# One accumulation for tokens k and 768-k: a shared second DFT, mirrored tiles, and their stores

## The chip, the cores and the metric

The kernel runs on one core of one Trainium2 chip. The metric is the device time of one execution in microseconds (us), some 1.8 us more than the profile's span. Times are medians over several executions. On one core the fast state is recognised by comparison with the other runs of the same kernel; two runs of the kernel before, one at 391.51 us with a granted clock of 0.667 (in the round of experiment 9) and one at 294.96 us (experiment 10), fell in the slow state and are not used in any ratio.

In the views, PE is TensorE (matmuls) and PEld its weight loads, DVE is VectorE, ACT ScalarE, POOL GpSimd, and SP the engine that issues the plain stores; SPq is its queue of DMAs. A bank is a part of PSUM, the memory in which matmuls accumulate. The granted clock (PEclk) is the share of TensorE's full clock that the profile shows as granted. A scatter is a store that takes the address of each row from a table. To land is to be complete in memory.

## The reference, cut to what matters

The first part is attention over blocks that a Sinkhorn-normalised matrix mixes (4 batches, 8 heads, 768 tokens, 64 columns a head). Its output x, 768 tokens of 512 columns per batch, goes through this:

```python
    X = np.fft.fft(x, axis=1)            # over 768 tokens
    X = np.fft.fft(X, axis=2)            # over 512 columns
    u = x + np.real(X)
    un = (u - mean(u)) / sqrt(var(u) + 1e-06)          # per token
    return u + np.maximum(un @ w_ch1, 0.0) @ w_ch2     # 512 -> 2048 -> 512
```

The real part has a symmetry: X[768-k, m] is X[k, 512-m]. Tokens k and 768-k therefore have the same spectrum with its columns reversed.

## The kernel before

A Python list scheduler fixes the order on every engine before launch, from cost estimates that each operation is added with. The 768 tokens are six tiles of 128 rows; tiles 0 to 2 are group 0 and tiles 3 to 5 are group 1, and a group goes through the MLP as one. Each tile has a buffer u that lives from the second DFT, through the statistics and the MLP, to the store of the result; there are six, so the next batch's u can be written only when this batch's store has landed.

```python
    many("u", 6, [128, DM], F32)                # six u buffers
    P.pool("pf", banks[0:5])                    # PSUM: five banks, and three for the MLP
    P.pool("pm", banks[5:8])
    ...
    def dft2(b, g):
        ...
        for tt in range(3):
            T = 3 * g + tt
            ps, u, st = Buf("pf"), Buf("u"), Buf("st")
            ...
            def f(_, one=one, ps=ps, T=T):
                for c in range(4):
                    one(c)                                        # 4 matmuls of 256 columns
                nc.tensor.matmul(ps.ap, lt[:, 128 * T:128 * T + 128], rb,
                                 start=False, stop=True, ...)     # 1 of 512 columns
            P.add(pe(mm(256, 4) + mm(512) + 0.05), f, ..., w=[ps, u], tag="dft2")
            P.add({"DVE": (0.6, 0.69)}, ... V.scalar_tensor_tensor(u ... rt ... ps),  tag="u")
            # then bn_stats and bn_aggr on DVE, four small operations on POOL ("ln"),
            # then un on DVE or ACT, its transpose by DMA, and the MLP of the group

    def mlp(b, g, pr_pe, pr_v):
        ...                                    # 16 blocks: 4 matmuls of 384 columns, then relu
        for tt in range(3):
            ...                                # 16 matmuls of 512 columns into one bank
            P.add({"DVE": (0.6, 0.69)}, lambda _, u=u, ps=ps:
                  V.tensor_tensor(u.ap, ps.ap, u.ap, op=ALU.add), ..., tag="res")
            P.add({"SP": (0.1, 2.3)}, lambda _, u=u, T=3 * g + tt:
                  nc.sync.dma_start(out_v[b, T], u.ap), r=[(u, 1)], w=[],
                  prio=pr_v, tag="out")        # 128 rows of 2 KB
```

## Time and profile before

| | before |
|---|---|
| median of 3 runs | 291.64 us (290.91 to 291.75) |
| profiled span, granted clock | 287.7 us, 0.994 |
| matmuls | 2332, TensorE busy 262.3 us |
| landing of a 128-row store | 2.0 us |
| start of the last residual addition to the end | 3.86 us |

The prediction below shows the lines that carry this.

### The profile page before, as it was taken

What the parts mean: (1) busy time and instruction counts of PE and PEld (TensorE: products, weight loads), DVE (VectorE), ACT (ScalarE), POOL (GpSimd) and SP (SyncE); (2) the same over time, 40 slices, a digit from 0 to 9 for tenths busy, and PEclk for the clock granted to TensorE, in tenths of its full rate; (3) what the DMA queues carried; (4) which work ended last, traced back from release to release, by engine and by line L of the source; (5) the groups of instructions that cost most, each with busy time, mean ns of one, the idle gap of its engine ahead of it and who ended that gap; (6) DMA issues with size and microseconds to landing.
All of it is one profiled execution on the core that took longest, in us unless ns stands there. A gap on an engine that the chain in (4) does not pass through costs nothing.

```text
span 287.7 us, 5848 instructions
## 1 busy us (share of the span) xinstructions
PE 262.3 (91%) x2332; PEld 159.9 (56%) x2332; DVE 174.4 (61%) x395; ACT 155.9 (54%) x315; POOL 54.1 (19%) x91
## 2 busy tenths in 40 slices
PE   0489987798999998999999999999999999999994
PEld 0258866655576565544576556456645645645541
DVE  4688999999999979971459863044514314302011
ACT  2688989738779737780369117316803712722700
POOL 8973300014900370200020002000200200200000
PEclk9997999999999999999999999999999999999999
DMA  7999999910991299330111220311111022021102
GB/s 115 220 263 240 214 209 212 218 44 2 151 154 27 21 217 123 63 79 32 48 46 44 13 106 8 54 73 43 46 59 62 9 55 110 11 46 73 39 0 109
DMA packets 43025, 26.32 MB, mean 91 GB/s; under 512 B 29834, under 2 KB 38552, under 8 KB 42996
## 3 DMA queue, kind: packets, MB, share of 16 engines
q0 software_dynamic: 22576, 15.16, 35.0%
q1 hardware_dynamic: 20422, 10.78, 14.1%
q8 instruction: 18, 0.29, 0.4%
q14 instruction: 9, 0.07, 0.1%
HBM read 28.95 MB, written 6.29 MB: 122 GB/s over the span
## 4 chain that ended last, share of the span: by engine, by line
PE 70%; DVE 17%; DMA 6%; issue 2%; ACT 2%; POOL 1%; DVEq 0%; ACTq 0%; POOLq 0%
PE bank L1177 28%; PE bank L1156 26%; DMA hr<-in_v_dram 4%; PE bank L1068 3%; PE bank L1015 3%; DVE rt L964 3%; PE bank L854 2%; DVE vsf L626 2%; DMA out_dram<-u 2%; DVE eb L930 2%; PE bank L1075 2%; PE bank L690 2%; PE bank L909 2%; PE bank L949 1%; DVE pmt L981 1%
## 5 line engine op out<-in xcount | busy, mean ns | idle before, releaser
L1168 ACT ACTIVATE hr<-bank 128x384 f16<-128x384 f32 x112 | 54.9, 490 | 84.0 <-PE bank L1156 83.6
L1156 PE MATMUL bank<-ut,w1sb 128*128 128x384 f16 x512 | 92.2, 326 | 0.0
L1177 PE MATMUL bank<-w2sb,hr 128*128 128x512 f16 x384 | 88.0, 379 | 0.0
L1156 PEld LDWEIGHTS <-w1sb 128*128 128x128 f16 x512 | 48.1, 98 | 32.9
L1177 PEld LDWEIGHTS <-hr 128*128 128x128 f16 x384 | 36.9, 98 | 41.2
L1185 DVE TENSOR_TENSOR u<-bank,u 128x512 f32<-128x512 f32 x24 | 16.5, 689 | 62.2 <-PE bank L1177 62.0
L1083 DVE SCALAR_TENSOR_TENSOR u<-rt,bank 128x512 f32<-128x512 f16 x24 | 16.1, 681 | 30.0 <-PE bank L1075 24.0
L918 ACT ACTIVATE ex<-bank 96x384 f32<-96x384 f32 x64 | 27.9, 487 | 9.8 <-PE bank L909 9.2
L1096 POOL TENSOR_SCALAR mv<-mv 128x3 f32<-128x3 f32 x8 | 2.0, 252 | 160.4 <-DVE mv L1091 148.4
L932 ACT ACTIVATE eb<-ex,negone 96x384 f16<-96x384 f32 x36 | 21.4, 617 | 0.1
L949 PE MATMUL bank<-vsf,eb 97*128 97x65 f16 x384 | 16.4, 193 | 2.6 <-DVE rt L964 1.0
L949 PEld LDWEIGHTS <-eb 97*128 97x128 f16 x384 | 14.8, 97 | 5.2 <-issue 2.2
L964 DVE TENSOR_TENSOR rt<-bank,rz 128x384 f16<-128x384 f32 x32 | 17.5, 550 | 0.3
L442 POOL DMA_DIRECT2D kq<-in_q_dram x20 | 16.4, 846 | 1.7 <-DMA kq<-in_q_dram 1.2
L1089 DVE BATCH_NORM_STATS2 st<-u 128x6 f32<-128x512 f32 x24 | 16.0, 684 | 0.2
L884 PE MATMUL bank<-pack,qr 128*128 128x128 f16 x48 | 4.8, 245 | 12.0 <-ACT qr L626 11.5
L626 ACT CAST vsf<-bank 96x512 f16<-96x512 f32 x16 | 11.9, 793 | 4.1 <-PE bank L690 3.3
L1116 ACT ACTIVATE un<-u,nm,ny 128x512 f16<-128x512 f32 x14 | 11.3, 810 | 3.8 <-DMA ut<-un 2.2
L690 PE MATMUL bank<-bdv,vcx 128*128 128x128 f16 (+1 forms) x128 | 12.5, 225 | 0.1
L854 PE MATMUL bank<-bdk,kq 128*64 128x128 f16 x192 | 10.6, 227 | 2.1 <-DVE bdk L602 0.8
L909 PE MATMUL bank<-qt,ks 64*128 64x96 f16 x256 | 11.4, 207 | 1.2 <-DVE u L1083 0.5
L626 DVE CAST vsf<-bank 96x512 f16<-96x512 f32 x16 | 11.7, 777 | 0.9 <-PE bank L693 0.8
(115 smaller groups left out, 323.8 us busy)
## 6 DMA issues: line engine op xcount, KB each, us to landing
out_dram<-u SPq DMA_DIRECT2D x24, 256.0 KB, 2.0
kq<-in_k_dram POOLq DMA_DIRECT2D x8, 384.0 KB, 6.3
w1sb<-in_moe_w_ch_dram POOLq DMA_DIRECT2D x4, 512.0 KB, 16.0
w2sb<-in_moe_w_ch_dram POOLq DMA_DIRECT2D x4, 512.0 KB, 19.0
kq<-in_q_dram POOLq DMA_DIRECT2D x4, 384.0 KB, 11.5
hr<-in_v_dram POOLq DMA_DIRECT2D x2, 768.0 KB, 11.0
kq<-in_v_dram POOLq DMA_DIRECT2D x2, 768.0 KB, 21.7
kq<-in_q_dram POOLq DMA_DIRECT2D x16, 96.0 KB, 5.7
```

What stands on the lines that cost most here:

```text
L442: o = P.add({eng: c}, lambda _: e.dma_start(dst, src), r=r, w=w, prio=prio, nbytes=nbytes, tag="load", after=after)
L626: (nc.scalar.copy if e == "ACT" else V.tensor_copy)(dst, src)
L690: nc.tensor.matmul(o, vcx[:, 96 * d:96 * d + m], bd, start=True, stop=(t == 1))
L909: nc.tensor.matmul(pss[h2].ap[:, BLK * j:BLK * j + BLK], ks.ap[rows, 4 * g + j, :], qt.ap[rows, c0:c0 + BLK])
L918: nc.scalar.activation(ex.ap, pss[h2].ap[0:96, 0:384], AF.Exp, scale=SCALE),
L932: nc.scalar.activation(ed, src, AF.Identity, bias=negone[0:96])
L949: nc.tensor.matmul(po.ap[:, 65 * T:65 * T + 65], eb.ap[:, e0:e0 + 128], vsf[:, vi:vi + 65], start=(n == 0), stop=(n == 1), skip_group_chec ...
L964: P.add({"DVE": (0.45, 0.56)}, lambda _: V.tensor_tensor(rt.ap[:, :, D * h:D * h + D], po3()[:, :, 0:D], rz.ap[:, :, None].broadcast_to([1 ...
L1156: nc.tensor.matmul(ps.ap[:, 0:GT], w1sb[:, c, 128 * fc:128 * fc + 128], ut.ap[:, c, :], start=(c == 0), stop=(c == 3))
L1168: nc.scalar.activation(hr[g][:, fc, :], ps.ap[:, 0:GT], AF.Relu)
L1177: nc.tensor.matmul(ps.ap, hr[g][:, fc, 128 * tt:128 * tt + 128], w2sb[:, fc, :], start=(fc == 0), stop=(fc == 15))
L1185: V.tensor_tensor(u.ap, ps.ap, u.ap, op=ALU.add),
```

## The change

Its intent is to take work from TensorE. Tiles 3 and 4 hold the mirrors of tiles 0 and 1, row for row, so they need not be accumulated again: one closing matmul, onto the bank that tile 0 or 1 has left in PSUM, exchanges the tokens' own part, and DVE reads that bank with its columns reversed. The first DFT is folded by s and -s, with fewer and longer matmuls. Mirrored rows run downwards in the output, so group 1 is stored by scatter, and tile 2 becomes tokens 257 to 383 and token 0, which is stored in two pieces. The MLP order of the last batch is turned round as well. The core of the diff, with cuts:

```diff
+TOK = [list(range(1, 129)), list(range(129, 257)),
+       list(range(257, 384)) + [0], list(range(767, 639, -1)),
+       list(range(639, 511, -1)), list(range(511, 383, -1))]
 ...
+            if T in (3, 4):
+                ps = banks_of[b, T - 3]
+                def f(_, ps=ps, T=T):
+                    nc.tensor.matmul(
+                        ps.ap, lt[:, LTD + 128 * (T - 3):LTD + 128 * (T - 2)],
+                        rb, start=False, stop=True, skip_group_check=True)
+                P.add(pe(mm(512) + 0.03), f, r=lts, w=[ps, u], tag="dft2")
 ...
+                    rev = bass.AP(
+                        tensor=p_.tensor, offset=p_[:, 511:512].offset,
+                        ap=[p_.ap[0], [-1, 255], [-256, 2]])
 ...
-            P.add({"SP": (0.1, 2.3)}, lambda _, u=u, T=3 * g + tt:
-                  nc.sync.dma_start(out_v[b, T], u.ap), r=[(u, 1)], w=[],
-                  prio=pr_v, tag="out")
+            def f(_, u=u, T=3 * g + tt):
+                t0 = TOK[T][0]
+                if T < 2:
+                    nc.sync.dma_start(out[b, t0:t0 + 128, :], u.ap)
+                elif T == 2:
+                    nc.sync.dma_start(out[b, t0:t0 + 127, :], u.ap[0:127])
+                    nc.sync.dma_start(out[b, 0:1, :], u.ap[127:128])
+                else:
+                    i = 3 * b + T - 3
+                    nc.gpsimd.indirect_dma_start(
+                        out.rearrange("b s m -> (b s) m"),
+                        bass.IndirectOffsetOnAxis(ap=rows[:, i:i + 1],
+                                                  axis=0), u.ap, None)
+            P.add({"SP": (0.1, 2.3)} if g == 0 else {"POOL": (1.2, 3.5)}, f,
+                  r=[(u, 1), "rows"], w=[], prio=pr_v, tag="out")
 ...
-            mlp(b, g, 100.0 + 10 * (2 * b + g), -300.0)
+            mlp(b, g, 100.0 + 10 * (2 * b + (g if b < B - 1 else 1 - g)), -300.0)
```

## The prediction

> **What bounds the kernel now.** I read the page first (engine shares, then the 40 slices), then busy time by stretches, then the chain of waits, then the timeline around one hand-over between batches. Shares and slices:
>
> ```profile
> PE 262.3 (91%) x2332; PEld 159.9 (56%) x2332; DVE 174.4 (61%) x395; ACT 155.9 (54%) x315; POOL 54.1 (19%) x91
> ...
> PE   0489987798999998999999999999999999999994
> ...
> DVE  4688999999999979971459863044514314302011
> ```
>
> The second row is PE, the third DVE: up to slice 16 (about 115 us) DVE is full and PE has holes; from slice 17 on PE is full. The stretches say it in us (PE, PEld, DVE, ACT, POOL):
>
> ```profile
> 40.00:60.00 20.00, 15.57 (x272) 12.74 (x267) 19.87 (x51) 17.67 (x40) 0.00 (x0) 1.00 1.08 198
> ...
> 120.00:140.00 20.00, 20.00 (x152) 10.09 (x150) 9.93 (x20) 10.18 (x22) 0.25 (x1) 1.00 0.21 57
> ...
> 180.00:200.00 20.00, 20.00 (x112) 10.76 (x111) 5.08 (x10) 6.80 (x14) 0.00 (x0) 1.00 0.23 57
> ```
>
> So the end is set by PE work left from about 117 us, provided that nothing keeps PE waiting there. The chain of waits gives the rate of each kind of PE work in that stage (start, us, what, how many):
>
> ```profile
> 155.82 0.91 PE bank L949 x24
> ...
> 191.46 0.44 PE bank L1068 x4
> 192.12 0.44 PE bank L1068 x4
> ...
> 200.36 1.70 PE bank L1015 x18
> ...
> 207.15 7.77 PE bank L1177 x36
> ```
>
> That is attention-times-value (L949) 0.91/24 = 38 ns; second DFT (L1068) 0.44 us for four 256-column matmuls, with 0.66 us from tile to tile, so 0.22 us for the closing 512-column one; first DFT (L1015) 1.70/18 = 94 ns for 193 columns; second MLP layer (L1177) 216 ns.
>
> The hand-over matters most. When the last tile of MLP group (1,0) is stored, its u buffer is refilled by batch 2, and all that normalises batch 2 hangs on that. Timeline of DVE, then POOL, then PE:
>
> ```profile
> 170.50 0.69 DVE L1185 TENSOR_TENSOR u<-bank,u 128x512 f32<-128x512 f32 x1 [0.75 <-PE bank L1177]
> ...
> 174.41 0.69 DVE L1083 SCALAR_TENSOR_TENSOR u<-rt,bank 128x512 f32<-128x512 f16 x1 [1.62 <-PE bank L1075]
> 175.13 0.69 DVE L1089 BATCH_NORM_STATS2 st<-u 128x6 f32<-128x512 f32 x1
> ```
> ```profile
> 176.13 0.23 POOL L1096 TENSOR_SCALAR mv<-mv 128x3 f32<-128x3 f32 x1 [24.98 <-DVE mv L1091]
> ```
> ```profile
> 181.37 7.93 PE L1177 MATMUL bank<-w2sb,hr 128*128 128x512 f16 x36
> 189.13 0.81 PE L1156 MATMUL bank<-ut,w1sb 128*128 128x384 f16 x4
> ```
>
> The refill at 174.41 waited for PE, not for the store, because a store lands fast:
>
> ```profile
> out_dram<-u SPq DMA_DIRECT2D x24, 256.0 KB, 2.0
> ```
>
> And after the last residual add only one such store remains:
>
> ```profile
> 283.84 0.69 DVE L1185 TENSOR_TENSOR u<-bank,u 128x512 f32<-128x512 f32 x1 [2.76 <-PE bank L1177]
> 284.56 0.33 SPq L1188 DMA_DIRECT2D out_dram<-u  x1
> ```
>
> **What the Trainium skill says.** (1) "DMA: Bandwidth & Descriptors", section "Why a DMA increments its semaphore by 16 and not by 1": a DMA runs on the largest k of at most 16 engines that divides the slowest dimensions of both sides, and a 127-partition tile issued from SP gets k = 1. All stores in this trace have 128 rows, so it cannot agree or disagree. (2) The same page, "Specifications": about 27 GiB/s for one engine. The stretch holding only the last store fits:
>
> ```profile
> 284.90:286.70 1.80, 0.00 (x0) 0.00 (x0) 0.00 (x0) 0.00 (x0) 0.00 (x0) 1.00 0.38 146
> ```
>
> 0.38 x 16 engines x 1.8 us = 10.9 engine-us for 128 rows of 2 KB, 85 ns a row, 24 GB/s. (3) The same page, "Anatomy of one DMA": a POOL-issued DMA costs about 2 us fixed, mostly the write receipt; the 2.0 us landing of SP's stores is of that size. (4) "Perfetto Trace Analysis", "DMA Instruction — SWDGE (GPSIMD)": the POOL interval is descriptor generation only. Here these take 0.53 to 1.0 us each.
>
> **The change part by part.**
>
> PE. Tiles 3 and 4 of each batch lose four 256-column matmuls each: 2 x 0.44 = 0.88 us per batch. The first DFT keeps its columns (3 x 386 against 6 x 193) in fewer, longer matmuls. At 384 columns this trace has 162 ns, so about 164 ns at 386: a chain goes from 566 to 2 x 164 + 2 x 94 = 516 ns (three chains) or 492 ns (two), 0.30 us per batch. Attention gains one 38 ns matmul per head, 0.30 us per batch. Counted in the stage where PE is full: mirrored tiles of batches 1 to 3, 2.64; first DFT of batches 2 and 3, 0.60; heads of batch 3, minus 0.30. Gain 2.9 us.
>
> DVE. Per batch, by the formula n/rate + about 0.15 us that the rows give: out go 4 yr copies (1.0), a third of ee, fo, oo, fq (4.1 becomes 2.8); in come 2 sign-folded sums (0.9), 3 two-column fix-ups (0.5), and half of 6 rv copies (0.6). Net near -0.4 us. The changed build's order has, before the first un, one more norm, em1 and vsf eviction and two fewer ks evictions than before; the sum comes out within 0.2 us. So no gain in the front.
>
> The group-0 stores. Tile 2 now holds tokens 257 to 383 and 0, so it is stored as 127 rows plus 1 row from SP. By (1) the 127 rows go to one engine: 127 x 85 ns = 10.8 us (9.0 at 27 GiB/s), in place of the 8 x 85 = 0.7 us inside the 2.0 us landing. Estimated landing 10.5 to 12, say 11.5 us. The scheduler's program still assumes 2.3. DVE and ACT are in order. From the residual add of tile 2 (end of its PE work = 0): add 0.7, store landed 12.2, u 12.9, statistics 13.7, POOL's four ops (1.8 us in the trace) 15.5, first un 16.1, and in the changed order the relu of the 15th MLP block stands behind that un on DVE: 16.6. PE until then has 6 + 7 blocks of 0.65, one DFT tile 0.66 and one 0.86 us quarter of a tile: it runs out at 10.0, since the next bank is the one that relu frees. Stall 6.6 us, for batches 1 to 2 and 2 to 3 alike. For 0 to 1, DVE has 4.1 us of other work before it meets the wait and PE reaches a blocked relu at about 7.5, freed at about 14.2: 6.5 us. Sum 19.7 us.
>
> The scatters. All three of a group go to the whole of out, so in the build each waits for the one before to land, and POOL stands. One period: about 1.2 us generation (estimate: 0.5 to 1.0 for plain ones plus reading indices) plus 2.2 landing = 3.5 us. Mid-run, adds of group 1 came at 187.7, 188.5 and 195.3, the refill of its third tile at 199.7; scatters would land at 192, 195.4 and 199.5: hidden. At the end they are not: swapping the last two groups does not help, because in the changed build's order group (3,1) is still last. Its tiles finish 4.3, 3.5 and 0 us before PE's end; scatters start at -3.6, -0.1 and +3.4, the last lands at +6.9, where the old store landed at 0.7 + 2.3 = 3.0. Cost 3.9 us.
>
> Sum: 291.6 - 2.9 + 19.7 + 3.9 = 312.3 us.
>
> **The rivals.** (a) The 127-row store is spread over many engines after all. For: nothing in this trace shows k. Against: the skill names exactly this shape. Then 291.6 - 2.9 + 3.9 = 292.6, the same. (b) The scatters become the wait that counts: at 5 us a period the third refill comes 3.7 us late at up to three hand-overs and the tail grows by about 8 rather than 3.9: 320 or more. Against: generation has been under 1 us. (c) PSUM: two of five banks stay held from group 0 to group 1 of a batch. For: the hold spans about 30 us of attention of the next batch. Against: the build's order has attention in the same slots between MLP blocks, and PE has MLP work there. 0 to 2 us. (d) The reversed reads lose DVE's faster modes. Reversed f16 reads do not (ee: 1542 elements in 0.97 us); f32 ones are unproven: 14 em1 of 0.2 us, under 3 us, in the DVE-bound front. (e) PE's saving alone counts, and the tail is hidden: 289; it needs both stores to land as the scheduler assumes.
>
> **Range and chances.** I put 0.85 on the single engine. Within it, landing between 10 and 12.5 us moves the sum by 1.5 us per us and hand-over, 305 to 317; rival (b) reaches beyond. Without it 290 to 296. I take 311, range 295 to 319; faster 0.04, within 2% 0.14, slower 0.82.
>
> **What would show it.** Right: the 127-row issue lands in about 11 us while 128-row ones keep 2; DVE's u of tile 2 idles 6 us or more on the out store; PE has three holes of about 6 us near 115, 182 and 240; PE's second-DFT instructions drop from 96 to 64 of 256 columns; after the last residual add about 7 us remain. Wrong: if that issue lands in 2 to 4 us, the main step falls. If DVE idles on scatters instead, (b) was right. If PE's holes have ACT or DVE busy before them rather than idle, (c) or (d).

## More of the kernel before

In the list of waits (who waited for what: us in total, times, longest us) DVE's wait for u on an earlier store was small (three waits, 6.0 us, the longest 4.0):

```profile
DVE u L1083 <- DMA out_dram<-u: 6.0, 3, 4.0
```

## The result, and the profile after

The changed kernel takes 323.48 us (321.9 to 324.59, 4 runs) beside 291.27 us for the kernel before (4 runs): the ratio is 1.1101, with an interval of 1.1048 to 1.1154. A ratio here is the mean time of one kernel's fast runs over the mean of the other's fast runs of the same rounds, so it is not quite the ratio of the medians. The change was predicted to be slower, and it is, but by 32 us where the prediction had about 20 and a range that ended at 319.

Read first the page of the changed kernel: busy time, then the slices of TensorE and of its granted clock.

```profile
PE 269.7 (84%) x2284; PEld 158.4 (49%) x2284; DVE 172.4 (54%) x405; ACT 158.4 (49%) x323; POOL 66.9 (21%) x104
...
PE   0599878979999993899999990999999189999990
...
PEclk9977999998999998599999998799999769999997
```

There are 48 matmuls fewer, yet TensorE is busy for longer. Its row has three new holes, in slices 15, 24 and 31 (counted from 0), and below each hole, or just after it, the clock row drops. Span less busy time grew from 25.4 to 52.4 us. The list of waits names the holes (TensorE's, then DVE's):

```profile
PE bank L1274 <- DVE hr L1262: 16.9, 2, 8.5
...
PE bank L952 <- DVE u L1160: 7.1, 1, 7.1
```
```profile
DVE u L1160 <- DMA out_dram<-u: 34.2, 4, 13.0
```

Holes of 7.1, 8.4 and 8.5 us sum to 24.0 us, and behind them DVE waits up to 13.0 us for a store of `out` to land, where the kernel before had 6.0 us in all. The timeline of one hand-over shows the links (start us, us, engine, line, operation):

```profile
183.24 0.69 DVE L1282 TENSOR_TENSOR u<-bank,u 128x512 f32<-128x512 f32 x1 [0.35 <-PE bank L1274]
183.96 0.25 SPq L1289 DMA_DIRECT2D out_dram<-u  x1
184.26 4.20 SPq L1290 DMA_DIRECT2D out_dram<-u  x1
196.91 0.69 DVE L1160 SCALAR_TENSOR_TENSOR u<-rt,bank 128x512 f32<-128x512 f16 x1 [12.99 <-DMA out_dram<-u]
...
200.92 0.55 DVE L1262 TENSOR_SCALAR hr<-bank 128x384 f16<-128x384 f32 x1
...
201.52 2.72 PE L1274 MATMUL bank<-w2sb,hr 128*128 128x512 f16 x6 [8.42 <-DVE hr L1262]
```

L1289 issues the 127 rows, L1290 the single row. The u of the next batch starts 12.95 us after the first issue; statistics, POOL's four operations, un and the relu follow, and TensorE starts again at 201.52. Two things stand out that were not predicted: the issue of the single row holds SP's queue for 4.20 us, and the stretches after the restart (PE, PEld, DVE, ACT, POOL busy, then the granted clock, DMA share, GB/s) run at half clock:

```profile
194.00:196.00 2.00, 0.00 (x0) 0.00 (x0) 0.00 (x0) 0.00 (x0) 0.00 (x0) 1.00 0.07 26
...
202.00:204.00 2.00, 2.00 (x6) 0.66 (x5) 0.00 (x0) 0.42 (x1) 0.00 (x0) 0.50 0.53 107
204.00:206.00 2.00, 2.00 (x8) 0.84 (x7) 0.00 (x0) 0.39 (x1) 0.00 (x0) 0.74 0.31 62
206.00:208.00 2.00, 2.00 (x12) 0.88 (x10) 0.00 (x0) 0.00 (x0) 0.00 (x0) 1.00 0.15 32
```

In the first of these lines nothing but the store moves: a DMA share of 0.07 is close to one engine of sixteen (0.0625), at 26 GB/s. In the second TensorE is never idle, and 6 matmuls fall in the 2 us; in the last, at full clock, 12 of the same kind do. The end of the run has changed as well:

```profile
313.62 0.69 DVE L1282 TENSOR_TENSOR u<-bank,u 128x512 f32<-128x512 f32 x1 [2.76 <-PE bank L1274]
313.89 0.97 POOL L1293 DMA_INDIRECT out_dram<-u,rows  x1 [2.53 <-DMA out_dram<-u,rows]
317.38 0.96 POOL L1293 DMA_INDIRECT out_dram<-u,rows  x1 [2.52 <-DMA out_dram<-u,rows]
```

Each scatter waits 2.5 us for the one before, and the run ends 8.5 us after the start of the last addition (322.1 less 313.62), against 3.86 before.

### The profile page after: what moved, and what is told of

Its sections match the earlier page's. It is cut to its first block, busy times and chain, and to the rows that moved or that the text cites. A ratio compares the mean times of both kernels' runs of the same rounds, so it can differ in the third digit from the quotient of the medians.

```text
span 322.1 us, 5799 instructions
## 1 busy us (share of the span) xinstructions
PE 269.7 (84%) x2284; PEld 158.4 (49%) x2284; DVE 172.4 (54%) x405; ACT 158.4 (49%) x323; POOL 66.9 (21%) x104
## 4 chain that ended last, share of the span: by engine, by line
PE 35%; issue 26%; DVE 19%; DMA 12%; POOL 5%; ACT 1%; POOLq 0%; SPq 0%; DVEq 0%
PE bank L1274 16%; PE bank L1253 12%; DMA out_dram<-u 5%; DMA hr<-in_v_dram 4%; DVE vcx L708 3%; DVE vsf L660 2%; DVE rt L1006 2%; DMA out_dram<-u,rows 2%; DMA kq<-in_q_dram 2%; POOL kq L472 2%; DVE st L1186 1%; POOL ny L1196 1%; PE bank L897 1%; DVE u L1160 1%; DVE ks L660 1%
## 5 line engine op out<-in xcount | busy, mean ns | idle before, releaser
L1274 PE MATMUL bank<-w2sb,hr 128*128 128x512 f16 x384 | 91.8, 391 | 16.9 <-DVE hr L1262 16.9
L1265 ACT ACTIVATE hr<-bank 128x384 f16<-128x384 f32 x115 | 56.3, 490 | 80.7 <-PE bank L1253 80.3
L1253 PE MATMUL bank<-ut,w1sb 128*128 128x384 f16 x512 | 94.8, 334 | 0.7 <-ACT ut L660 0.7
L1253 PEld LDWEIGHTS <-w1sb 128*128 128x128 f16 x512 | 49.5, 99 | 35.9 <-issue 3.7
L1160 DVE SCALAR_TENSOR_TENSOR u<-rt,bank 128x512 f32<-128x512 f16 x12 | 8.0, 685 | 40.1 <-DMA out_dram<-u 34.2
L1293 POOL DMA_INDIRECT out_dram<-u,rows x12 | 12.1, 1011 | 81.7 <-DVE u L1282 61.5
L1213 ACT ACTIVATE un<-u,nm,ny 128x512 f16<-128x512 f32 x15 | 12.2, 812 | 29.6 <-POOL nm L1202 20.9
L1172 DVE SCALAR_TENSOR_TENSOR u<-rt,bank 128x510 f32<-128x510 f16 x12 | 8.1, 680 | 16.3 <-PE bank L1138 8.8
L952 PEld LDWEIGHTS <-ks 64*128 64x128 f16 x256 | 7.1, 97 | 15.6 <-issue 14.8
L897 PE MATMUL bank<-bdk,kq 128*64 128x128 f16 x192 | 11.7, 244 | 1.1 <-ACT ks L660 0.6
## 6 DMA issues: line engine op xcount, KB each, us to landing
kq<-in_q_dram POOLq DMA_DIRECT2D x4, 384.0 KB, 11.5
hr<-in_v_dram POOLq DMA_DIRECT2D x2, 768.0 KB, 10.8
```

The source lines that it names most:

```text
L897: nc.tensor.matmul(ps.ap[64 * h2:64 * h2 + 64, 128 * r3:128 * r3 + 128], k16[:, 2 * hl + h2, 3 * half + r3, :], bdk[:, 2 * hp + h2].rearra ...
L952: nc.tensor.matmul(pss[h2].ap[:, BLK * j:BLK * j + BLK], ks.ap[rows, 4 * g + j, :], qt.ap[rows, c0:c0 + BLK])
L1253: nc.tensor.matmul(ps.ap[:, 0:GT], w1sb[:, c, 128 * fc:128 * fc + 128], ut.ap[:, c, :], start=(c == 0), stop=(c == 3))
L1265: nc.scalar.activation(hr[g][:, fc, :], ps.ap[:, 0:GT], AF.Relu)
L1274: nc.tensor.matmul(ps.ap, hr[g][:, fc, 128 * tt:128 * tt + 128], w2sb[:, fc, :], start=(fc == 0), stop=(fc == 15))
```

## The experiments

The theory (A): the 127-row store runs on one DMA engine and holds u; the holes and the slow restarts follow from it; the scatters cost only at the end. The rivals: the single-row store or the scatters hold u (B); the shared PSUM banks or the reversed reads cost the time; the clock falls for a reason of its own.

### 1. The same rows, cut so that they spread

```diff
-                    nc.sync.dma_start(out[b, t0:t0 + 127, :], u.ap[0:127])
+                    nc.sync.dma_start(out[b, t0:t0 + 112, :], u.ap[0:112])
+                    nc.sync.dma_start(out[b, t0 + 112:t0 + 127, :],
+                                      u.ap[112:127])
```

> The changed kernel with the 127-row store of the tile that straddles the middle cut into 112 rows and 15 rows (the single row of token 0 stays its own store); nothing else moves. Theory A (the 127-row store is not spread: [...] one DMA engine carries 254 KB, lands about 13 us after its issue, holds u, and TensorE then idles 7 to 8.5 us three times and restarts at half clock): both pieces land within about 2 to 3 us, the three holes (24.0 us) and the half-clock stretches (about 7 us) go, so 322 - 31 = 291 us, between 289 and 296. Theory B (the one-row store, whose issue holds the SP queue 4.1 us, or the scatters on the POOL queue, are what u waits for): the one-row store and the scatters are unchanged, so the holes shrink by a third at most and the time stays above 312 us.

Measured: 292.93 us, ratio to before 1.0063 (0.9996 to 1.013), against 1.1101 for the changed kernel. The 112 rows land 2.3 us after their issue. All three holes and all the half-clock stretches behind them are gone:

```profile
PE   0389888897999999999999999999999999999980
...
PEclk9999997999999999999999999999999999999996
```

The single row is still stored by an instruction of its own, and its issue no longer holds the queue:

```profile
L1292 SPq DMA_DIRECT2D out_dram<-u x4: 231/238/249, 114.8 to 263.3; - x4
```

Theory B falls: scatters, single row, shared banks and reversed reads are all still there. The difference of the two profiled spans, 33.8 us, splits into 23.0 us of idle TensorE (52.4 less 29.4) and 10.8 us of busy time (269.7 less 258.9) for the same 2284 matmuls. The latter is clock: 6.9 us behind the holes (worked out below), and most of the rest in the front, where the profiled run of the changed kernel had 10.2 us at half clock and this one 3.4.

### 2. A dose in between

```diff
+                    nc.sync.dma_start(out[b, t0:t0 + 122, :], u.ap[0:122])
+                    nc.sync.dma_start(out[b, t0 + 122:t0 + 127, :],
+                                      u.ap[122:127])
```

> The changed kernel with the same store cut into 122 rows (61 times 2: two engines) and 5 rows (five engines). A dose between the changed kernel (one engine) and the cut at 112 (sixteen). Theory A: the large piece moves 250 KB over two engines, so it lands after about 5.5 to 7 us instead of 13; a wait of 13 us then falls to 5.5 to 6.5 us and the TensorE holes of 7.1, 8.4 and 8.5 us fall to between 0 and 2 us each. With holes that short there is no restart at half clock if the clock theory (a restart at half rate follows a long idle stretch only) is right: 322 - 24 + 3 - 7 = 294 us, between 290 and 300. If instead the clock falls after any hole, 297 to 303 us. Theory B: above 312 us.

Measured: 304.99 us, ratio 1.0499 (1.0442 to 1.0555). The order of the three cuts is as theory A has it, but the size was missed: I expected at most 300.

```profile
182.00:184.00 2.00, 2.00 (x15) 1.18 (x13) 0.00 (x0) 1.12 (x3) 0.00 (x0) 1.00 0.13 49
```
```profile
186.25 0.69 DVE L1160 SCALAR_TENSOR_TENSOR u<-rt,bank 128x512 f32<-128x512 f16 x1 [8.13 <-DMA out_dram<-u]
...
190.88 8.79 PE L1274 MATMUL bank<-w2sb,hr 128*128 128x512 f16 x40 [3.58 <-DVE hr L1262]
```

The store now moves 49 GB/s at a DMA share of 0.13, two engines' worth, and u is written 8.1 us after the issue at 178.15 instead of 12.95. That is more than the 5.5 to 7 us that I had worked out, so the holes are 2.2, 3.58 and 3.25 us, 9.0 in all. The clock gives a second result. The 40 matmuls after the hole of 3.58 us take 8.79 us and the clock stays at 1.00 (after the hole of 3.25 us too); after 8.4 us of idleness, in the changed kernel, the same 40 took 10.52. Only the first hand-over has a stretch at 0.50, though its hole was the shortest, 2.2 us; there TensorE was busy for only 1.34 us of the stretch from 122 to 124 us and 0.45 us of the next two. So the length of the hole alone does not decide it.

### 3 and 4. That part alone in the kernel before, and its control

```diff
+                if T == 2:
+                    nc.sync.dma_start(out_v[b, T][0:127], u.ap[0:127])
+                    nc.sync.dma_start(out_v[b, T][127:128], u.ap[127:128])
+                else:
                     nc.sync.dma_start(out_v[b, T], u.ap)
```

> The kernel before with only one thing of the change: its third tile of each group of tokens 0 to 383 is stored as 127 rows and 1 row, with the same two instructions; token order, second DFT and plain stores of all other tiles stay. Theory A: the tile's u buffer is held about 11 us longer than before, so the same three holes appear in the matmuls (batches 1, 2, 3), each 5 to 9 us, with half-clock restarts: 291 + 20 to 32 = 311 to 323 us. If the loss came from the change's other parts (scatters, shared accumulations that hold PSUM banks), this kernel takes 291 to 294 us.

The control has 64 in place of 127 in those lines, and 64 rows in the second piece:

> Control for the one before: the same tile stored by two instructions too, but as 64 and 64 rows, which spread over all engines. Theory A: 290 to 293 us, the same as before within 1%. If a second store on the queue is itself what delays u, it loses as much as the cut in 127 and 1: above 305 us.

Measured: 322.07 us for 127 and 1, ratio 1.107 (1.0997 to 1.1143); 290.06 us for 64 and 64, ratio 0.9986 (0.9931 to 1.0041). In the first:

```profile
PE bank L1156 <- DVE hr L1165: 8.8, 1, 8.8
PE bank L854 <- DVE u L1083: 8.8, 1, 8.8
PE bank L1177 <- DVE hr L1165: 8.0, 1, 8.0
```

Three holes, 25.6 us, in a kernel without scatter, shared banks, mirrored tiles or reversed reads. This one store of the change, alone, gives a ratio within 0.3% of the changed kernel's (1.107 beside 1.1101). A second instruction on the queue is harmless when its rows spread.

### 5. Useless work in the holes

```diff
                             w2sb[:, fc, :], start=(fc == 0), stop=(fc == 15))
+                    if g == 1 and b in (1, 2) and tt == 0 and qd == 0:
+                        for _ in range(34):
+                            nc.tensor.matmul(ps.ap[0:96], zz, w2sb[:, 0, :],
+                                             start=False, stop=False)
```

> The changed kernel, all stores as they are, with useless work added: in the second and third hole, right after the four matmuls that precede it, 34 matmuls with all-zero weights (96 columns, 512 wide) accumulate zero onto the same bank; the result stays right. 34 x 0.216 = 7.3 us of them fit inside holes of 8.4 and 8.5 us. Clock theory (after a long idle stretch TensorE restarts at half clock): the granted clock after these two holes stays at 1.00, the 40 matmuls after them take 8.65 us instead of 10.5 and 10.7, and the kernel is about 4 us faster although it does more: ratio to before 1.096 instead of 1.110, 319 to 320 us. The first hole keeps its half-clock stretch. Rival (the low clock comes from something else, for example a power budget or the order of work): adding matmuls changes nothing or costs time, 323 to 326 us, with 0.50 still in the windows after the holes.

Measured: 320.13 us, correct, ratio 1.1006 (1.0958 to 1.1054): about 3 us faster with 68 matmuls more. The timeline:

```profile
192.64 7.50 PE L1280 MATMUL bank<-w2sb,zz 128*96 128x512 f16 x34
201.24 8.79 PE L1275 MATMUL bank<-w2sb,hr 128*128 128x512 f16 x40 [1.10 <-DVE hr L1263]
```

The restart comes at the same moment as before (201.24 beside 201.52), and the 40 matmuls run at full clock: 8.79 us in place of 10.52, and in the third hole 8.79 in place of 10.72. So it is the idleness that lowers the clock: the same holes, filled, leave it at 1.00. The gain is a little under the 4 us expected.

### 6. Plain stores for the mirrored tiles (wrong)

```diff
-                    nc.gpsimd.indirect_dma_start( ... rows[:, i:i + 1] ... )
+                    nc.sync.dma_start(out[b, t0 - 127:t0 + 1, :], u.ap)
```

> The changed kernel with the 127 rows cut into 112 and 15, and the six mirrored tiles' scatters replaced by plain stores of 128 rows to the same block of tokens, at the same places in the order. Wrong on purpose: the rows of tokens 384 to 767 come out in reversed order, since a store with a negative row step was refused by the compiler. It isolates what the scatter costs. If the scatters cost only at the end (three in a chain, 3.5 us apart, tail 4.7 us longer), this takes about 4 us less than the cut at 112 alone: 288 to 289.5 us, ratio to before 0.990 to 0.995. If they cost in the middle too, more than 6 us less.

Measured: 286.99 us, ratio 0.988 (0.9844 to 0.9915); the result is wrong (relative error 0.297). That is below the 288 to 289.5 us that I expected. The scatters cost 1.8% (1.0063 less 0.988), 5.3 us: between the two answers that I had set. The profiled spans, 288.3 and 283.8, differ by 4.5 us, and the tails account for all of it (8.47 us from the start of the last addition to the end, against 3.67). So I read no cost in the middle; the 1 us that the medians leave over is within the noise of the two ratios (0.7% and 0.35% either way, measured in different rounds). What remains is the change's own gain: 1.2% of 290.85 is 3.5 us (2.5 to 4.5 by the interval), where the prediction had 2.9. It is clear of 1.

### 7. The tiles of the last group one after the other

```diff
                       w=[ps], prio=pr_pe + 0.1, tag="ff2",
+                      after=last if (b, g) == (3, 1) else ())
+            last = [P.ops[-1]]
```

> The changed kernel with the 127 rows cut into 112 and 15, and in the last group alone the second product's matmuls of tile A all before those of B, and B's before C's (before, A and B are interleaved and end 0.9 us apart). Correct. Tile A then ends 2.6 to 3 us earlier, so its scatter starts about 3 us earlier, and the chain of three scatters is no longer what is waited for, only the last one: 2.5 to 3 us less than the cut at 112 alone, 289 to 290.5 us, ratio to before 0.993 to 1.000. If the tail is not a chain of scatters, nothing changes.

Measured: 290.37 us, correct, ratio 0.9982 (0.9946 to 1.0019), as expected. The last scatter now starts 1.2 us after the start of the last addition:

```profile
281.61 0.69 DVE L1285 TENSOR_TENSOR u<-bank,u 128x512 f32<-128x512 f32 x1 [2.76 <-PE bank L1275]
282.81 0.96 POOL L1298 DMA_INDIRECT out_dram<-u,rows  x1 [2.53 <-DVE u L1285]
```

The tail is 5.9 us instead of 8.5. It was a chain of scatters.

### 8. The single row first

```diff
-                    nc.sync.dma_start(out[b, t0:t0 + 127, :], u.ap[0:127])
                     nc.sync.dma_start(out[b, 0:1, :], u.ap[127:128])
+                    nc.sync.dma_start(out[b, t0:t0 + 127, :], u.ap[0:127])
```

> The changed kernel with only the order of two stores swapped: the one row of token 0 first, then the 127 rows. If the 4.1 us for which the one-row store's issue held the SP queue is a consequence of the 127 rows ahead of it on the same engine, the one-row issue now takes 0.25 us and the holes shrink only by what the pair landed later because of the row, 0 to 1 us each: 320 to 323 us. If the one-row store itself is slow and is what u waits for, its issue still takes 4 us and the time stays the same or rises.

Measured: 322.95 us, ratio 1.1128 (1.1073 to 1.1182), the same as the changed kernel's 1.1101. The issue of the row takes 0.25 us, that of the 127 rows 0.24 us, and the holes are 7.3, 8.6 and 8.6 us. So the 4 us for which the row's issue held the queue came of the 127 rows ahead of it, and cost nothing here.

### 9. The orientation turned round

In this version tiles 0 to 2 are held in descending order and the mirrored tiles in ascending order, so group 0 is scattered and group 1, which ends last, is stored plainly; the token tables, the attention windows, the column order of the first DFT and the stores were changed for it.

```diff
+TOK = [list(range(128, 0, -1)), list(range(256, 128, -1)),
+       [0] + list(range(383, 256, -1)), list(range(640, 768)),
+       list(range(512, 640)), list(range(384, 512))]
 ...
-                if T < 2:
+                if T > 2:
+                    t0 = TOK[T][0]
                     nc.sync.dma_start(out[b, t0:t0 + 128, :], u.ap)
```

> The change turned around, to keep its gain and lose both costs: the tiles of tokens 0 to 383 are held in descending order (tile 2 as token 0, then 383 down to 257) and the mirrored tiles are then ascending, so group 1, which ends last, is stored by plain 128-row stores, and the three tiles of group 0 by scatter, with the odd row 0 in the third scatter; no 127-row store is left. Should be correct. If the scatters cost only at the end, as the 1.8% between the plain mirrored stores and the cut at 112 says, this runs as fast as the plain mirrored stores but right: 286 to 289 us, ratio to before 0.983 to 0.995, with no hole over 1.5 us in the matmuls and the end 3.5 to 4.2 us after the start of the last addition. If scatters also cost in the middle of the run (in group 0 they hold u and the POOL queue before the next batch's statistics), holes appear and it takes 291 us or more.

Measured: 292.81 us, correct, ratio 1.0072 (1.0016 to 1.0129). The hope failed, in the way named last. The tail is right (3.96 us), but a hole of 5.1 us appeared at the first hand-over:

```profile
108.68 1.03 POOL L1290 DMA_INDIRECT out_dram<-u,rows  x1 [0.30 <-issue]
```
```profile
119.53 0.69 DVE L1160 SCALAR_TENSOR_TENSOR u<-rt,bank 128x512 f32<-128x512 f16 x1 [6.18 <-DMA out_dram<-u,rows]
```
```profile
DMA to landing us min/median/max: 2.7/2.8/10.7
```

A scatter of batch 0 took 10.7 us to land instead of 2.7. It was issued behind the loads of batch 2's q and k on the same POOL queue, and in the stretch from 110 to 120 us the DMA share was 2.34 (the times of the packets in flight, added, were more than the 16 engines' time). That it waited behind those loads is argued from the order and not tested. The hole of 5.1 us was followed by a stretch at half clock too (122 to 124 us: 0.50).

### 10. The middle tile and its mirror exchanged

On top of the seventh run, groups became tiles (0, 1, 5) and (3, 4, 2), so that the last store is a plain one:

```diff
+TG = ((0, 1, 5), (3, 4, 2))
-            T = 3 * g + tt
+            T = TG[g][tt]
```

> A version meant to keep the change's gain: the cut at 112, the tail order of the seventh run, and the middle tile and its mirror exchange groups: group 0 is now tiles 0, 1 and 5, group 1 is tiles 3, 4 and 2, so the group that ends last has two scatters first and ends with plain stores of tile 2 (112, 15 and 1 rows). Should be correct. The last scatter is then issued about 3.5 us before the last addition, and what ends the kernel is a plain store: 1.5 to 2 us less than the tail order alone (290.4 us, ratio 0.998), so 288 to 289.5 us, ratio to before 0.987 to 0.995. One scatter per batch now lies in group 0; in batch 0 it comes at about 113 us, after the loads of batch 2's q and k have been issued. If it lands late behind them, as the second scatter of batch 0 did in the ninth run (10.7 us instead of 2.7), u waits and the gain is lost: 291 to 294 us.

Measured: 292.36 us, correct, ratio 1.0072 (1.002 to 1.0124): the 288 to 289.5 us expected were missed, for a reason that stays in part open. The tail is 4.3 us, as meant (285.80 to 290.1), and no scatter lands later than 3.2 us after its issue, so what was feared did not happen. But the last addition starts at 285.80, 4.2 us later than in the seventh run. The first MLP matmul already comes 1.8 us later (72.0 against 70.2); before it this profiled run had 6.8 us at half clock and that of the seventh 3.4, worth 1.7 us at most. The other 2.4 us are not explained: the scheduler gave this version another order throughout.

No correct version beat the kernel before by more than the scatter of the runs: the best is the seventh, equal to it. The sixth shows what the idea is worth if reversed rows could be stored for nothing, 1.2%. Plain stores with a negative row step, in memory or on chip, could not be built (no run shows it).

## Why the prediction was right or wrong, point by point

- **The single engine: right.** Experiments 1 to 4 show it from both sides. The Trainium skill, "DMA: Bandwidth & Descriptors", section "Why a DMA increments its semaphore by 16 and not by 1", has a rule (the largest number up to 16 that divides the rows) by which 112 rows go to 16 engines, 15 to 15, 122 to 2 and 127 to 1; the DMA shares of 0.07 for 127 rows and 0.13 for 122 agree, and the counts for 112 and 15 were not measured.
- **The landing, and so the stall: mis-sized.** The prediction had the store landing about 11.5 us after issue; the next u started 12.95 us after it. The rate was right: windows with nothing but the store have 25 to 26 GB/s, about 80 ns a row where it had 85. What it left out lies at the ends: after the issue at 183.96 the first traffic shows between 184.5 and 185.0, until 187.5 all traffic together is only 8 to 37 GB/s, the last shows after 196.25, and u starts at 196.91. TensorE ran out about 10 us after the end of the tile's work, as predicted (193.1 less about 183.2), but restarted 18.3 us after it instead of 16.6. Per hole that is 7.1, 8.4 and 8.5 us for 6.5, 6.6 and 6.6: 24.0 instead of 19.7.
- **The restart at half clock: missing.** This is the step that failed: the sum counts a hole at its length alone and has TensorE at full clock, 216 ns a matmul, right after it. Of the 11 us missing, 6.9 lie here, against 4.3 in the holes themselves. The Trainium skill, "TensorE: Matmul & The Clock Gate", section "Part 1: The HAM clock gate (the "warmup" mystery)", says that TensorE falls to half its clock after an idle window of about 3.4 us and regains it after a busy one of about the same length; I had not carried it into the sum. The traces agree in that the clock is at 0.50 after holes of 5.1 us and more. They do not agree with a fixed time from the start of a hole: in the third hole TensorE had stopped at 250.68, and the clock fell 2.2 us later:

```profile
252.50:252.75 0.25, 0.00 (x0) 0.00 (x0) 0.00 (x0) 0.00 (x0) 0.00 (x0) 1.00 0.06 25
252.75:253.00 0.25, 0.00 (x0) 0.00 (x0) 0.00 (x0) 0.00 (x0) 0.00 (x0) 0.68 0.06 25
```

  In the first hole it took 3.3 us and in the second 5.1, and full clock came back 6.4, 3.5 and 3.9 us after the restarts. The six moments at which the clock changed (126.55, 136.79, 198.23, 205.05, 252.84 and 263.08 us) are all whole multiples of 3.413 us apart, so it matters too where a hole lies against these steps. The 40 matmuls after the second and third hole lost 10.52 - 8.79 = 1.73 and 10.72 - 8.79 = 1.93 us. After the first hole TensorE ran from 130.43 to 136 at 0.50 and to 138 at 0.80, 6.4 us at half clock or 3.2 us lost (an estimate: TensorE is taken to be the limit throughout). Sum 6.9 us; experiment 5 gives back 3 of the 3.7 us of the second and third.
- **The scatters: right in kind, a little small.** The period is 3.5 us as predicted, hidden in mid-run, and the tail grew by 4.6 us (8.5 less 3.86) where 3.9 was predicted. Experiments 6 and 7 confirm it. The scatters took 0.96 to 1.15 us on POOL where the prediction estimated 1.2.
- **TensorE's saving: right in size.** 2.9 us predicted, 3.5 us in experiment 6, which is the net gain of everything but the stores. The rivals on PSUM and reversed reads fall with it: everything they speak of is in a kernel that is 1.2% faster than before.
- **Slips in the working, none of which decided it.** The first stall is 14.2 - 7.5 = 6.7 us, not 6.5. DVE's items add to -0.3 us a batch, not -0.4 (DVE's busy time fell by 2.0 us in all). The 1.5 us per us of landing, from which the range comes, is not derived: the three holes grew by 0.6, 1.8 and 1.9 us for 1.45 us. Of the signs named, the matmuls of the second DFT did fall from 96 to 64; the three holes came at 123, 193 and 251 us rather than 115, 182 and 240.
- **The sum.** 291.3 - 3.5 + 24.0 + 6.9 + 4.6 = 323.3 us, beside 323.48 measured. Of the 11 us by which the prediction's own sum, 312.3, fell short, 6.9 are the clock, 4.3 the landing and 0.7 the tail, less 0.6 of gain and 0.3 of the lower base.

## What to carry to other kernels

Before a tile changes its row count, factor it: a store of 127 rows cost 11% of a whole kernel, and 112 and 15 in its place cost nothing. When a change opens a hole in TensorE's work, add to its length what the restart costs, 1.7 to 3.2 us here. Two holes of 3.25 and 3.58 us were free of that, but one of 2.2 us with little work around it was not, so no safe length was found. A buffer that only a store frees is on the critical path as soon as the store is slow, however idle the DMA engines look.

## What the Trainium skill lacked or had wrong

- "DMA: Bandwidth & Descriptors" gives the rule for k, and the runs agree with it. I found nothing there on what the issuing queue does behind a one-engine store: the next store's issue held SP's queue for 3.9 to 4.2 us, 3.3 to 3.7 in the third run, and 0.24 us when that store came first or when the rows ahead of it were spread.
- The same page, section "Specifications", has about 27 GiB/s for one engine, which is 29 GB/s; 26 GB/s was measured for one and 49 for two, 10 to 16% less.
- I found no page with the time of an indirect store: 0.96 to 1.15 us on POOL for 128 rows in the changed kernel, and 2.7 us from issue to landing, but 10.7 us once behind loads on the same queue. Three in a row to one output run 3.5 us apart.
- "TensorE: Matmul & The Clock Gate", section "Part 1: The HAM clock gate (the "warmup" mystery)", has the fall after at least one idle window of about 3.4 us. That is too strict as it stands: the clock fell 2.2 us after the last matmul in the third hole, and in experiment 2 after a hole of 2.2 us, with TensorE busy for 1.8 of the 4 us from 122 to 126. Holes of 3.25 and 3.58 us left it at 1.00, holes of 5.1 us and more did not. That zero-weight matmuls count as activity, and keep the clock at 1.00 through an 8 us hole, I found on no page.
- No page has the speed of an operand read backwards ("Vector Engine (DVE) Microarchitecture Reference" lists a negative step as not measured). Reading an fp32 PSUM bank with reversed columns took DVE no longer: 685 ns for 510 columns reversed, 686 ns for 512 in order; the two columns left over take an operation of their own, 154 ns.
